# A transformer block on one core: heads loaded one by one, uses booked further behind transfers, program order from V on, and splits ahead of additions

## The chip, the cores and the metric

The kernel runs on one core of a Trainium2 chip. The metric is the device time of one execution in microseconds (us), as a median over runs. Five engines have a part in it. In the profile TensorE is PE, with its weight loads listed apart as PEld; VectorE is DVE, ScalarE is ACT, GpSimd is POOL, and SyncE, which here does nothing but issue DMAs, is SP. "SPq" and "ACTq" are rows of an engine's DMA issues.

## What is computed

```python
xn = layernorm(x)                                   # x: 2048 x 576
q, k, v = heads(xn @ wqkv)                          # 32 heads of 18
p = softmax(mask(q @ k.T * 18 ** -0.5))             # a row sees itself and the 255 before
s = (p @ v) @ wo
z = gelu(xn @ w_in)                                 # 2 x 2304 channels
z1, z2 = z[:, :2304], layernorm(z[:, 2304:])
g = silu((z1 * (w_sp @ z2 + b_sp)) @ w_out)         # w_sp: 2048 x 2048, along the sequence
out = x + s * g
```

Both branches take the normalised x. All data is fp32.

## The kernel before

**Number format.** Every large product is made of fp32r halves: `split` (lines 111 to 113) writes a rounded upper half with ACT (L112) and the remainder with DVE (L113), and TensorE multiplies upper by upper, upper by lower and lower by upper.

**Stages.** (1) Q and K: x is normalised and transposed, `qk_chunk` multiplies, and SP stores the rows to `st_d` in DRAM. (2) V (`v_matmuls`, L465 to L473): sixteen row blocks, two PSUM buffers `vps`; ACT copies each to `ve` (L472) and issues its store itself (L473). (3) z2 (L678): six column parts `pc` of sixteen row blocks `s`; ACT makes the Gelu (L698), and its own queue stores two blocks at a time to `z2_d`. Beside it GpSimd makes sums and differences of the quarters of w_sp (`sp_combos`, L610 to L627) for the spatial stage, which is a product of 2 x 2 blocks with seven multiplications instead of eight; they go to `sc_d`. The weights of the next column part come in three pieces (`load_z2`, `pieces`): each piece is loaded, and at the second next row block split. (4) The heads, with z1 between. (5) The spatial product. (6) The product with wo, and the output.

**Heads.** The work is cut into 16 units: four heads and one half of the sequence each. A unit is two pairs of heads; a pair has one of five SBUF slots `att0` to `att4`, with the first head in partitions 0 to 63 and the second in 64 to 127: a part with two heads' Q, and a part with both heads' K. `load_pair` issues eight DMAs for a pair, four for each head (L361 to L364, from `st_d`). Both pairs that follow, the second pair of the next unit and the first of the one behind it, are loaded in one go at the start of each unit. Three streams are interleaved on TensorE:
- `row_max` (a matmul L394, then DVE's maximum L398) runs some 42 steps ahead and finds each row's maximum, which goes through DRAM (`m_d`) into the slot.
- `scores` (L526) takes the items of the unit, each a block of keys of one head: 32 in a unit of the first half, 40 in the second. ACT takes the exponential into `pt` (L530). `pv` multiplies by V (L549).
- `fill` hands out the matmuls of z1 (L447), 14 to a group of 512 columns. ACT copies a group to `z1o` (L450), SP stores it (L376). The weights of the next 128 channels come with `load_z1` (L425, tile `z1raw`) and are split into `z1wh` and `z1wl` (L483 in the profile, where the jobs are called) when they are booked in `extras`.

`finish` ends a unit: a row of the PV product holds the denominators. SP brings them to a tile `den` (L598), DVE inverts (L574), SP sends them to `r_d` (L575) and spreads them over the partitions (`rp`, L579), DVE multiplies (L583), and SP stores four heads to `o_d` (L589).

**Order.** In these stages the kernel sets the order itself. `manual_schedule` names the engines that run in the order of the program; from V through z2 these are PE, POOL and DVE (`ENGINES`), while ACT and SP are put in an order by the compiler's own schedule; in the heads they are all five (`HEADS`). Inside that, `after(ns, fn)` books a piece of work a number of nanoseconds on, by a clock that `spend` moves by an estimate for each matmul; `tick` issues what has come due. `extras` is a list of jobs for DVE and ACT, of which `extra` issues some. An engine does what it was given strictly in this order, so a late input stops everything behind it.

**Spatial.** 168 steps m: three groups g of 384 channels, seven products n, eight steps s. A step is 18 matmuls into six PSUM banks `acc` (L964). SP loads a tile of w_sp or of its combinations (`load_w`, tile `spr`, L205), ACT and DVE split it into `sph` and `spl` and the z2 tile into `zh` and `zl` (`split_step`, L210 in the profile), two steps ahead. `pump` loads z2 blocks (`zr`) and normalises them (ACT, and DVE at L159 to L165). When a product ends (s = 7) `evict` adds or copies the six banks; the additions of the second product are at L913, the copies of the first at L925. It also books in `lazy` the loads of z1 (`z1t`, L881), their Gelu (L889), the products with the gate and the stores to `y_d`; `run_lazy(4)` issues four of these in each step. All five engines follow the program here.

One place a sentence can't say, the end of a spatial step:

```python
            if s == 7:
                evict(g, n)
            load_w(m + 4)
            if m:
                split_step(m + 2)
...
            pump(2 if len(units) > 8 and (m < 4 or m % 3 == 0) else 1)
            run_lazy(4)
```

Of the kernel before, what the change touches and what calls it, by code (L numbers as in the profile page):

```python
# [44 lines left out]
GAP = 7  # L45
TAIL = 66
HEAD = 6
# [14 lines left out]
def kernel(  # L62
# [163 lines left out]
    with ExitStack() as early:  # L226
# [108 lines left out]
        with ExitStack() as ph:  # L335
# [17 lines left out]
            def load_pair(p):  # L353
                u, a = divmod(p, 2)
                g, half = UNITS[u]
                q0 = half * HS
                k0, kn = (0, HS) if half == 0 else (HS - 256, HS + 256)
                for j in (2 * a, 2 * a + 1):
                    h, b = 4 * g + j, 64 * (j % 2)
                    q, k = f32(q_of(u, j)), f32(k_of(u, j))  # L360
                    sp.dma_start(q[b:b + 36, :], st_d[0, 0:36, h, q0:q0 + HS])  # L361
                    sp.dma_start(k[b:b + 18, :kn], st_d[1, 18:36, h, k0:k0 + kn])
                    sp.dma_start(q[b + 36:b + 56, :], st_d[0, 18:38, h, q0:q0 + HS])
                    sp.dma_start(k[b + 18:b + 54, :kn], st_d[1, 0:36, h, k0:k0 + kn])  # L364

            waiting, seen = [], []
# [69 lines left out]
            def z1_matmuls():  # L436
                nxt = z1_first.pop()
                for f in range(FH // P):
# [3 lines left out]
                    for c in range(NC):  # L442
# [3 lines left out]
                        for n, (w, r) in enumerate(pl):  # L446
# [7 lines left out]
                            if c == 1 and n == 7 and f + 1 < FH // P:  # L454
                                extras.append(nxt[2])
# [111 lines left out]
            def finish(u, ou):  # L567
# [5 lines left out]
                def invert():  # L573
                    dve.reciprocal(den, den)  # L574
                    after(600, lambda: sp.dma_start(r_d[u].rearrange("h (a b) -> (h a) b", b=HS // 32), den))  # L575
                    after(2800, spread)

                def spread():
                    sp.dma_start(rp, r_d[u].unsqueeze(1).to_broadcast([4, 32, HS]))  # L579
                    after(9500, lambda: queue([divide]))  # L580
# [5 lines left out]
                def store():  # L586
                    for i in range(4):
# [11 lines left out]
                after(3600, lambda: queue([invert]))  # L599

            def sp_combos(stack):
# [13 lines left out]
                for n, (q, cs) in enumerate(steps):  # L615
# [9 lines left out]
                    yield  # L625
                    for k, t in enumerate((a22, a11, a21, a12)):
                        sp.dma_start(sc_d[k, q, :, cs], t)  # L627
# [3 lines left out]
            order.enter_context(tc.manual_schedule(engines=ENGINES))  # L631
            with ExitStack() as gate:
                def load_z2(pc):
# [26 lines left out]
                for pc in range(6):  # L660
# [7 lines left out]
                    if pc == 3:  # L668
                        load_pair(0)
                        load_pair(1)  # L670
                    if pc == 4:
                        load_pair(2)
                    for s in range(NS):
# [8 lines left out]
                        if (pc * NS + s) % 3 != 2:  # L682
# [33 lines left out]
            with ExitStack() as heads:  # L716
# [19 lines left out]
                for u in range(NU):  # L736
                    g, half = UNITS[u]
                    tick()
                    if u == NU - 1:
# [12 lines left out]
                        for q in range(8):  # L752
                            prep.append(partial(act.activation, z0[:, q], z0[:, q], AF.Identity,
                                                scale=rstd2[:, q:q + 1], bias=nmr2[:, q:q + 1]))
# [7 lines left out]
                    for t, (s, j) in enumerate(items):  # L762
                        f = (t + 1) / len(items)
                        scores(u, *s, j)
# [20 lines left out]
                        if u == NU - 1 and t >= 12 and prep:  # L785
# [9 lines left out]
                fill(1)  # L795
                work.close()
                wpools[2] = open_pool(sets, "w2", side="right")
                load_w(2)
                fill(12)
# [29 lines left out]
    with ExitStack() as ph:  # L829
# [124 lines left out]
        for m, (g, n, s) in enumerate(order_sp):  # L954
# [11 lines left out]
            if s == 7:  # L966
                evict(g, n)
# [6 lines left out]
            run_lazy(4)  # L974
            if s == 5:
# [154 lines left out]
```

## Time and profile before

| what | before |
|---|---|
| median of 3 runs (lowest, highest) | 2070.53 us (2068.66, 2072.85) |
| the profiled execution: its time, its span | 2066.54 us, 2064.8 us |
| mean granted TensorE clock | 0.979 |
| busy: PE, DVE, ACT, POOL | 94%, 51%, 43%, 14% |
| busy share of the DMA engines by SP's and ACT's own queues | 54.0%, 3.7% |
| Q and K up to | 174 us |
| V up to | 211 us |
| z2 up to | 457 us |
| heads and z1 up to | 1045 us |
| spatial product up to | 1796 us |

The span runs from the first to the last instruction of the profiled execution. A row of a timeline names the start, the length, the engine and the source line; what stands in brackets is the idle time of the engine ahead of that instruction, and what ended it. Tile names lose their numbers there: `att` is any of the five slots, `acc` any PSUM bank, `b` any of the buffers `b0` to `b5`.

### The profile page before, as it was taken

To read this page: it belongs to the slowest core of one execution; us is meant where nothing else is said; L and a number is where in the kernel's file an instruction comes from. 1 tells how busy PE (TensorE), PEld (TensorE's weight loads), DVE (VectorE), ACT (ScalarE), POOL (GpSimd) and SP (SyncE) were. 2 spreads that over 40 slices of the span, in tenths; PEclk is the share of its full clock that TensorE was granted. 3 is DMA by queue.
4 is the path that set the end of the run, shared out by engine and by line. 5 is a ranking of instruction groups with operands and counts; after the bars stand their busy time and mean duration, and the time that the engine had idled before them with its cause. 6 is when DMAs were issued, how large, how long until landed. Compare 5 with 4: busy or idle time off the path is not lost.

```text
span 2064.8 us, 30616 instructions
## 1 busy us (share of the span) xinstructions
PE 1948.8 (94%) x11096; PEld 1672.1 (81%) x11096; DVE 1058.7 (51%) x2258; ACT 897.4 (43%) x1655; POOL 285.6 (14%) x362
## 2 busy tenths in 40 slices
PE   6999999998988889989998998999999999999998
PEld 5888999996766667767586887788888877999998
DVE  6411323365655556556236675667775666533231
ACT  4212222224554446556655555555655344432221
POOL 5001556102222222223300000000000000000000
PEclk9999999999999999999999999999999999999999
DMA  8655899234454545545456667665784466764451
GB/s 244 172 143 168 289 337 327 100 96 120 127 138 113 132 122 144 139 124 141 142 194 200 209 231 245 215 218 197 262 278 159 153 211 228 243 209 141 151 161 54
DMA packets 218983, 375.57 MB, mean 182 GB/s; under 512 B 43216, under 2 KB 115792, under 8 KB 218704
## 3 DMA queue, kind: packets, MB, share of 16 engines
q1 hardware_dynamic: 201168, 344.94, 54.0%
q10 hardware_dynamic: 17664, 28.69, 3.7%
q8 instruction: 87, 1.43, 0.3%
q14 instruction: 64, 0.52, 0.1%
HBM read 260.45 MB, written 112.83 MB: 181 GB/s over the span
## 4 chain that ended last, share of the span: by engine, by line
PE 73%; DMA 14%; DVE 7%; ACT 3%; issue 2%; SPq 1%; ACTq 0%; POOL 0%; DVEq 0%; POOLq 0%
PE acc L964 24%; PE po L1057 11%; PE mm L678 10%; PE mm L447 8%; PE mm L306 5%; PE tps L526 3%; PE ops L549 3%; PE sp L394 3%; DMA att<-st_d 3%; PE vps L465 2%; DMA z1t<-z_d 2%; DMA den<-ou 2%; DMA z1raw<-in_w_z_dram 1%; DVE spl L210 1%; PE wops L1027 1%
## 5 line engine op out<-in xcount | busy, mean ns | idle before, releaser
L964 PE MATMUL acc<-sph,zh 128*128 128x512 f32 x1008 | 397.5, 394 | 22.0 <-ACT sph L210 22.0
L964 PE MATMUL acc<-spl,zh 128*128 128x512 f32 x1008 | 398.1, 395 | 5.9 <-DVE spl L210 5.8
L964 PE MATMUL acc<-sph,zl 128*128 128x512 f32 x1008 | 396.1, 393 | 0.0
L398 DVE CUSTOM_DVE_ANT_0 junk<-sp,band 128x384 bf16<-128x384 f32 (+1 forms) x512 | 272.1, 538 | 181.9 <-PE sp L394 178.2
L530 ACT ACTIVATE pt<-tps 128x384 f32<-128x384 f32 (+2 forms) x576 | 247.3, 439 | 176.6 <-PE tps L526 163.6
L447 PE MATMUL mm<-b,z1wh 128*128 128x512 f32 x648 | 258.7, 409 | 0.0
L964 PEld LDWEIGHTS acc<-sph,zh 128*128 128x128 f32 x1008 | 191.9, 190 | 65.1 <-ACT sph L210 24.9
L964 PEld LDWEIGHTS acc<-spl,zh 128*128 128x128 f32 x1008 | 191.7, 190 | 50.7 <-DVE spl L210 11.0
L210 DVE TENSOR_TENSOR spl<-spr,sph 128x1024 fp32r<-128x1024 f32 x166 | 203.2, 1224 | 57.3 <-ACT sph L210 56.5
L964 PEld LDWEIGHTS acc<-sph,zl 128*128 128x128 f32 x1008 | 191.9, 190 | 39.8
L526 PE MATMUL tps<-att 128*128 128x384 f32 (+1 forms) x576 | 193.7, 336 | 23.6 <-ACT pt L530 21.7
L394 PE MATMUL sp<-att 128*128 128x384 f32 (+1 forms) x512 | 177.1, 346 | 33.6 <-DVE mx L398 26.5
L678 PE MATMUL mm<-z2wh,b 128*128 128x384 f32 x720 | 194.0, 337 | 3.6 <-ACT zt L698 3.6
L210 ACT ACTIVATE sph<-spr 128x1024 fp32r<-128x1024 f32 x166 | 173.9, 1048 | 36.3 <-DMA spr<-sc_d 25.1
L210 ACT ACTIVATE zh<-b 128x384 fp32r<-128x384 f32 x144 | 74.9, 520 | 195.8 <-PE acc L964 195.8
L210 DVE TENSOR_TENSOR zl<-b,zh 128x384 fp32r<-128x384 f32 x144 | 80.1, 556 | 151.5 <-ACT zh L210 151.4
L1057 PE MATMUL po<-b,yh 128*128 128x288 f32 x896 | 152.4, 292 | 0.0
L526 PEld LDWEIGHTS tps<-att 128*128 128x128 f32 x576 | 112.6, 195 | 48.1 <-ACT pt L530 35.7
L447 PEld LDWEIGHTS mm<-b,z1wh 128*128 128x128 f32 x648 | 126.1, 195 | 27.9 <-issue 7.2
L533 POOL TENSOR_SCALAR_AFFINE_SELECT pt<-pt 128x512 f32<-128x512 f32 x128 | 83.1, 649 | 462.4 <-ACT pt L530 462.4
L447 PE MATMUL mm<-b,z1wl 128*128 128x512 f32 x360 | 147.0, 408 | 0.0
L699 DVE BATCH_NORM_STATS2 st<-zt 128x6 f32<-128x384 f32 x96 | 53.5, 560 | 170.9 <-ACT zt L698 170.9
(150 smaller groups left out, 2913.7 us busy)
## 6 DMA issues: line engine op xcount, KB each, us to landing
spr<-sc_d SPq DMA_DIRECT2D x96, 512.0 KB
spr<-in_w_sp_dram SPq DMA_DIRECT2D x72, 512.0 KB
zr<-z_d SPq DMA_DIRECT2D x136, 192.0 KB
st_d<-qkhl SPq DMA_DIRECT2D x72, 256.0 KB
z_d<-zt ACTq DMA_DIRECT2D x48, 384.0 KB
z_d<-z1o SPq DMA_DIRECT2D x72, 256.0 KB
z1t<-z_d SPq DMA_DIRECT2D x72, 256.0 KB
y_d<-z1t SPq DMA_DIRECT2D x72, 256.0 KB
```

The costliest lines, as they stand in the source:

```text
L210: job()
L306: pe.matmul(ps, w, r, start=n == 0, stop=n == len(pl) - 1)
L394: pe.matmul(ps[:, :w], q_of(u, j)[:, i * P:(i + 1) * P], k_of(u, j)[:, k0:k0 + w], start=True, stop=True)
L398: dve.tensor_tensor_reduce(out=junk[:, :w], in0=ps[:, :w], in1=band[:, m0:m0 + w], scale=1.0, scalar=-3.0e38, op0=ALU.add, op1=ALU.max, ac ...
L447: pe.matmul(ps, w, r, start=n == 0, stop=n == len(pl) - 1)
L526: pe.matmul(ps[:, :m * P], k_of(u, j)[:, (kb - base) * P:(kb - base + 1) * P], q_of(u, j)[:, (a - lo) * P:(a - lo + m) * P], start=True, s ...
L530: act.activation(pt[:, j, d0:d0 + n * P], ps[:, (qa - a) * P:(qa - a + n) * P], AF.Exp, scale=scale)
L533: pool.affine_select(out=pt[:, :, 0:P], in_=pt[:, :, 0:P], pattern=[[0, 4], [1, P]], compare_op=ALU.is_ge, fill=0.0, base=0, channel_multi ...
L549: pe.matmul(o_ps[c][32 * j:32 * j + 32, (lo - 4 * c) * P:(hi - 4 * c + 1) * P], vgs[u][:, kb - k0, j * VW:j * VW + 32], pt[:, j, (lo - kb) ...
L678: pe.matmul(ps[:, :ZW], r, wt, start=n == 0, stop=n == len(pl) - 1)
L964: pe.matmul(acc[j], z[:, ps], w[:, cs], start=s == i == 0 and n in OPENS, stop=s == 7 and i == 2, skip_group_check=True)
L1057: pe.matmul(po[i][:, a, :288], y[:, i * P:(i + 1) * P], w[:, a * 288:(a + 1) * 288], start=f == 0 and m == 0, stop=f == NF - 1 and m == 2)
```

## The change

1. `load_head` takes the place of `load_pair`. Of the same four heads that a unit loads, each is now issued ahead of an item of its own, t = 0, 4, 10 and 16 (`LOAD_AT`): first the two heads of the second pair of the next unit, then the two of the first pair of the unit behind it.
2. Bookings. The reciprocal is booked 8000 ns instead of 3600 behind the PV product's end (except in the last two units), the denominators' store 900 instead of 600 and the spreading 3000 instead of 2800 ns behind it, the division 12000 instead of 9500 (9000 in the last two units). The split of the next z1 weights is booked seven matmuls later. Sixteen instead of six z1 matmuls stand ahead of the first unit (`HEAD`).
3. From V on ACT and SP run in the order of the program too (`HEADS` instead of `ENGINES`). V's loop calls the pieces of z2's first weights itself; the pieces of the others are loaded two ahead of their split (three tiles in hand instead of one at a time); `sp_combos` has one more `yield` ahead of its stores and is called at seven of eight row blocks instead of two of three.
4. In the last unit z0 is normalised by DVE instead of ACT and these jobs begin at t = 8 instead of 12. Behind the heads the program fills until the last but one unit's stores are issued (`stored`).
5. In the spatial product `evict` moves from the front of a step's work to its end.

```diff
-            def load_pair(p):
-                u, a = divmod(p, 2)
+            def load_head(u, j):
                 g, half = UNITS[u]
...
-                            if c == 1 and n == 7 and f + 1 < FH // P:
+                            if c == 2 and n == 0 and f + 1 < FH // P:
                                 extras.append(nxt[2])
...
-                    after(600, lambda: sp.dma_start(r_d[u].rearrange("h (a b) -> (h a) b", b=HS // 32), den))
-                    after(2800, spread)
+                    after(900, lambda: sp.dma_start(r_d[u].rearrange("h (a b) -> (h a) b", b=HS // 32), den))
+                    after(3000, spread)
...
-                    after(9500, lambda: queue([divide]))
+                    after(12000 if u < NU - 2 else 9000, lambda: queue([divide]))
...
-                after(3600, lambda: queue([invert]))
+                after(8000 if u < NU - 2 else 3600, lambda: queue([invert]))
...
                     pool.tensor_tensor(a12, a12, a11, ALU.subtract)
                     yield
+                    yield
                     for k, t in enumerate((a22, a11, a21, a12)):
                         sp.dma_start(sc_d[k, q, :, cs], t)
...
-            order.enter_context(tc.manual_schedule(engines=ENGINES))
+            order.enter_context(tc.manual_schedule(engines=HEADS))
...
+                    def piece(c):
+                        raw = f32(zw.tile([P, 5, P], F32R, name=("z1wh", "z1wl")[c % 2]))
+                        sp.dma_start(raw, w_z2[:, :, pc * ZW + c * P:pc * ZW + (c + 1) * P])
+                        return raw
+
                     def pieces():
+                        raws = [piece(0)]
+                        yield
+                        raws.append(piece(1))
+                        yield
                         for c in range(3):
                             cs = slice(c * P, (c + 1) * P)
-                            raw = f32(zw.tile([P, 5, P], F32R, name=("z1wh", "z1wl")[c % 2]))
-                            sp.dma_start(raw, w_z2[:, :, pc * ZW + c * P:pc * ZW + (c + 1) * P])
+                            split(wh[:, :, cs], wl[:, :, cs], raws[c])
+                            if c == 0:
+                                raws.append(piece(2))
                             yield
-                            split(wh[:, :, cs], wl[:, :, cs], raw)
-                            yield
...
-                for _ in nxt[2]:
-                    pass
-                for _ in vm:
-                    pass
+                for n, _ in enumerate(vm):
+                    if n % 28 == 7:
+                        next(nxt[2], None)
...
-                        if (pc * NS + s) % 3 != 2:
+                        if (pc * NS + s) % 8 != 7:
                             next(combos, None)
...
-                    for p in (2 * u + 3, 2 * u + 4):
-                        if p < 2 * NU:
-                            load_pair(p)
+                    heads_at = {LOAD_AT[i]: (u + 1 + i // 2, (2, 3, 0, 1)[i]) for i in range(4)}
...
                         f = (t + 1) / len(items)
+                        if t in heads_at and heads_at[t][0] < NU:
+                            load_head(*heads_at[t])
                         scores(u, *s, j)
...
-            if s == 7:
-                evict(g, n)
             load_w(m + 4)
             if m:
                 split_step(m + 2)
...
             run_lazy(4)
+            if s == 7:
+                evict(g, n)
```

Three places show what it moves. The first is SP in the fifth unit, which starts at 595.18 us in the trace. Before, these rows stand behind twelve more head loads: `att_1207` is a slot, `z1raw` the next z1 weights, `den` the denominators of the unit before.

```order
L361 DMA att_1207<-st_d 36x1024
L362 DMA att_1207<-st_d 18x1024
L363 DMA att_1207<-st_d 20x1024
L364 DMA att_1207<-st_d 36x1024
L425 DMA z1raw<-in_w_z_dram 128x640
L376 DMA z_d<-z1o 128x512
L598 DMA den<-ou 128x1x32
L575 DMA r_d<-den 128x32
```

After, with the last load of the first head at the top (source lines of the changed kernel, one less here):

```order
L363 DMA att_1206<-st_d 36x1024
L424 DMA z1raw<-in_w_z_dram 128x640
L589 DMA o_d<-ou 18x1024 x4
L375 DMA z_d<-z1o 128x512
L360 DMA att_1206<-st_d 36x1024
L361 DMA att_1206<-st_d 18x1024
L362 DMA att_1206<-st_d 20x1024
L363 DMA att_1206<-st_d 36x1024
L598 DMA den<-ou 128x1x32
```

The z1 weights now stand behind four head loads and the denominators behind eight, where both stood behind sixteen; and the output stores of an earlier unit, `o_d`, have come between the two heads of the pair.

The second place is DVE where the spatial product's second product ends. Before, `cb` are the six additions, `zl` and `spl` the lower halves for a step ahead, `b` a z2 tile.

```order
L161 TENSOR_TENSOR b_11539<-b_11304,z_10577 128x384
L913 TENSOR_TENSOR cb<-acc_11028,b_11025 128x512
L913 TENSOR_TENSOR cb<-acc_11029,b_11025 128x512
L913 TENSOR_TENSOR cb<-acc_11030,b_11025 128x512
L913 TENSOR_TENSOR cb<-acc_11031,b_11025 128x512
L913 TENSOR_TENSOR cb<-acc_11032,b_11025 128x512
L913 TENSOR_TENSOR cb<-acc_11033,b_11025 128x512
L210 TENSOR_TENSOR zl<-b_11304,zh 128x384
L210 TENSOR_TENSOR spl<-spr,sph 128x1024
```

After (in the changed kernel's own line numbers, where L211 is the splits and L925 the additions):

```order
L211 TENSOR_TENSOR zl<-b_11292,zh 128x384
L211 TENSOR_TENSOR spl<-spr,sph 128x1024
L162 TENSOR_TENSOR b_11539<-b_11292,z_10577 128x384 x2
L925 TENSOR_TENSOR cb<-acc_11028,b_11025 128x512
L925 TENSOR_TENSOR cb<-acc_11029,b_11025 128x512
L925 TENSOR_TENSOR cb<-acc_11030,b_11025 128x512
L925 TENSOR_TENSOR cb<-acc_11031,b_11025 128x512
L925 TENSOR_TENSOR cb<-acc_11032,b_11025 128x512
L925 TENSOR_TENSOR cb<-acc_11033,b_11025 128x512
L211 TENSOR_TENSOR zl<-b_11292,zh 128x384
L211 TENSOR_TENSOR spl<-spr,sph 128x1024
```

The same six additions now stand behind the split and the normalisations of their own step, and ahead of the next step's split.

The third place is ACT where Q and K end and V begins. `qkhl` is the upper half of a Q or K group, `ve` the copy of a V group, `v_d` its store; `att_1205` and `z2wh` receive z2's weights. Before:

```order
L112 ACTIVATE qkhl<-mm 128x512 x4
L472 ACTIVATE ve<-vps 128x16x18 x2
L473 DMA v_d<-ve 128x621
L112 ACTIVATE qkhl<-mm 128x512
L112 ACTIVATE z2wh<-z1wl 128x5x128
L472 ACTIVATE ve<-vps 128x16x18 x2
L473 DMA v_d<-ve 128x621
L112 ACTIVATE att_1205<-z1wh 128x5x128
```

After:

```order
L471 ACTIVATE ve<-vps 128x16x18 x2
L472 DMA v_d<-ve 128x621
L113 ACTIVATE qkhl<-mm 128x512 x13
L113 ACTIVATE att_1205<-z1wh 128x5x128
L471 ACTIVATE ve<-vps 128x16x18 x2
L472 DMA v_d<-ve 128x621
L471 ACTIVATE ve<-vps 128x16x18 x2
L472 DMA v_d<-ve 128x621
```

The copies of V groups between the last Q and K groups are gone, and the copy of z2's first piece stands ahead of two V groups.

More of the change, by code (lines that the diff above doesn't have):

```diff
@@ L45 @@
 GAP = 7
+LOAD_AT = (0, 4, 10, 16)
 TAIL = 66
-HEAD = 6
+HEAD = 16
 _SHARE = [18 + 0.4 * (i >= 8) for i in range(16)]
@@ L357, in load_pair @@
                 k0, kn = (0, HS) if half == 0 else (HS - 256, HS + 256)
[L358 to L366, printed above, removed]
+                h, b = 4 * g + j, 64 * (j % 2)
+                q, k = f32(q_of(u, j)), f32(k_of(u, j))
+                sp.dma_start(q[b:b + 36, :], st_d[0, 0:36, h, q0:q0 + HS])
+                sp.dma_start(k[b:b + 18, :kn], st_d[1, 18:36, h, k0:k0 + kn])
+                sp.dma_start(q[b + 36:b + 56, :], st_d[0, 18:38, h, q0:q0 + HS])
+                sp.dma_start(k[b + 18:b + 54, :kn], st_d[1, 0:36, h, k0:k0 + kn])
+            waiting, seen, stored = [], [], set()
             clock = 0.0
@@ L586, in store @@
                 def store():
+                    stored.add(u)
                     for i in range(4):
@@ L668 @@
                     if pc == 3:
-                        load_pair(0)
-                        load_pair(1)
+                        for j in range(4):
+                            load_head(0, j)
                     if pc == 4:
-                        load_pair(2)
+                        for j in range(2):
+                            load_head(1, j)
                     for s in range(NS):
@@ L752 @@
                         for q in range(8):
-                            prep.append(partial(act.activation, z0[:, q], z0[:, q], AF.Identity,
-                                                scale=rstd2[:, q:q + 1], bias=nmr2[:, q:q + 1]))
+                            prep.append(partial(dve.tensor_scalar, z0[:, q], z0[:, q], rstd2[:, q:q + 1],
+                                                nmr2[:, q:q + 1], ALU.mult, ALU.add))
                         prep += split_jobs(0) + split_jobs(1)
-                    for p in (2 * u + 3, 2 * u + 4):
-                        if p < 2 * NU:
-                            load_pair(p)
+                    heads_at = {LOAD_AT[i]: (u + 1 + i // 2, (2, 3, 0, 1)[i]) for i in range(4)}
                     steps = steps_of(half)
@@ L784 @@
                             load_v(u + 1)
-                        if u == NU - 1 and t >= 12 and prep:
+                        if u == NU - 1 and t >= 8 and prep:
                             prep.pop(0)()
@@ L795 @@
                 fill(1)
+                while NU - 2 not in stored:
+                    fill(1)
+                    extra(1)
                 work.close()
@@ L798 @@
                 load_w(2)
-                fill(12)
+                fill(10)
                 split_step(2)
```

## The prediction

> **What bounds the kernel now.** The page first: TensorE (PE) is busy for 94% of the span, the others for half or less, so the time is PE's work plus the time in which PE waits or runs slowly.
>
> ```profile
> span 2064.8 us, 30616 instructions
> PE 1948.8 (94%) x11096; PEld 1672.1 (81%) x11096; DVE 1058.7 (51%) x2258; ACT 897.4 (43%) x1655; POOL 285.6 (14%) x362
> ```
>
> The windows view by stage: start:end, length, busy time of PE, PEld, DVE, ACT and POOL, then granted PE clock, DMA share, GB/s. The stages are z2, the heads and the spatial product:
>
> ```profile
> 211.00:457.00 246.00, 242.42 (x1387) 240.96 (x1386) 94.42 (x213) 56.31 (x112) 94.46 (x70) 0.99 0.66 233
> 457.00:1045.00 588.00, 528.73 (x3475) 406.74 (x3474) 315.62 (x1071) 321.36 (x747) 153.09 (x240) 0.96 0.49 132
> 1045.00:1796.00 751.00, 723.12 (x3183) 595.33 (x3182) 491.36 (x690) 391.60 (x582) 0.00 (x0) 0.98 0.65 216
> ```
>
> PE idles 3.6, 59.3 and 27.9 us there. The view of waits, over the whole span, says for what (total, times, longest); the rows of DVE and ACT, over the heads, name what stands behind two of them:
>
> ```profile
> PE sp L394 <- DVE mx L398: 26.5, 14, 4.4
> PE acc L964 <- ACT sph L210: 22.0, 6, 5.6
> PE tps L526 <- ACT pt L530: 21.7, 13, 6.1
> PE sp L394 <- DMA att<-st_d: 6.9, 7, 2.4
> PE acc L964 <- DVE spl L210: 5.8, 10, 0.8
> PE vps L465 <- ACT ve L472: 2.6, 1, 2.6
> DVE den L574 <- DMA den<-ou: 50.1, 9, 18.0
> ACT z1wh L483 <- DMA z1raw<-in_w_z_dram: 20.7, 5, 7.1
> ```
>
> One such stall, in the unit that starts at 595.18, by the timeline (start, length, engine, line; in brackets idle time before it and its releaser). SyncE (SP) issues sixteen head loads (the dots), then the z1 weights, and only then the denominators; DVE stands at the reciprocal, row maxima queue behind it, PE stops:
>
> ```profile
> 595.18 0.34 PE L526 MATMUL tps<-att 128*128 128x384 f32 x1
> 595.00 0.33 SPq L361 DMA_DIRECT2D att<-st_d  x1
> ...
> 605.44 0.57 SPq L598 DMA_DIRECT2D den<-ou  x1
> 610.41 0.35 DVE L574 RECIPROCAL den<-den 128x32 f32<-128x32 f32 x1 [4.61 <-DMA den<-ou]
> 611.23 0.69 PE L394 MATMUL sp<-att 128*128 128x384 f32 x1 [3.75 <-DVE mx L398]
> ```
>
> A stall costs more than its length. After 2.84 us of idling the granted clock is half for the next 3.4 us; around a stall of 1.79 us it is full:
>
> ```profile
> 508.45 0.56 PE L394 MATMUL sp<-att 128*128 128x384 f32 x1 [2.84 <-DVE mx L398]
> 508.62:512.03 3.41, 3.41 (x10) 3.04 (x11) 1.39 (x6) 1.56 (x4) 0.00 (x0) 0.50 0.57 137
> 542.67 0.44 PE L394 MATMUL sp<-att 128*128 128x384 f32 x1 [1.79 <-DVE mx L398]
> 541.00:546.00 5.00, 3.33 (x17) 3.00 (x18) 3.38 (x13) 2.88 (x7) 0.89 (x3) 1.00 0.66 193
> 641.74:648.56 6.82, 3.56 (x10) 3.17 (x11) 1.26 (x5) 3.07 (x7) 1.22 (x2) 0.50 0.28 76
> ```
>
> So a long stall loses 1.7 us more. From the stage clocks: heads 0.04 x 588 = 23 us withheld, spatial 0.02 x 751 = 15. Part of that falls on idle time (half of it in the last row, none in the 508 row), so I count four fifths: 19 and 12 us. In z2 it is 0.01 x 246 = 2, and V's one stall of 2.6 us adds about 1. With that stall, 93 us of idling and 34 of slow clock lie between V and the end of the spatial product; the rest of the kernel the change hardly touches.
>
> **The change, heads.** *Reciprocal.* It is booked 4.4 us later, and only eight of the sixteen head loads now stand in front of its DMA. DVE waited 50.1 us for it in nine places, 18.0 of them in the last unit, where nothing needs DVE: the other eight are 4.0 us on average (4.61 above). The two shifts together are more, so this stall goes, and with it nearly all of the 26.5 us. The z1 split moves seven z1 matmuls back, and its load is issued ahead of most head loads instead of behind all sixteen: of the 20.7 us that ACT waited for it, at most 7.1 at once, nothing should remain, and of PE's 21.7 little. HEAD = 16 covers the table switch at the start. In the last unit eight normalisations go from ACT to DVE, which has no row maxima left. The second pair of each unit, now loaded at t = 10 and 16, is first read near t = 24 of 32, eight items or some 8 us later, longer than any landing below: no cost. PE's own order is the same from the last head to the spatial product, so the wait for the last output stores costs nothing either.
>
> *What is late next.* The first row maximum of an even head needs the K rows of both heads of its pair: the slot's K tile is read on all 128 partitions. Here PE waited for the eighth load of the unit:
>
> ```profile
> 707.36 0.33 SPq L361 DMA_DIRECT2D att<-st_d  x1
> ...
> 711.31 0.29 SPq L364 DMA_DIRECT2D att<-st_d  x1
> 717.59 0.41 PE L394 MATMUL sp<-att 128*128 128x384 f32 x1 [1.22 <-DMA att<-st_d]
> 603.65 0.28 PE L394 MATMUL sp<-att 128*128 128x256 f32 x1
> 498.80 3.07 DMA att<-st_d
> L583 DVE TENSOR_TENSOR ou<-ou,rp 128x1024 f32<-128x1024 f32 x15 | 18.8, 1250 | 0.0
> ```
>
> It is needed 8.5 us after the unit's start (603.65 against 595.18). After the change the pair's second head stands behind t = 4 and, in seven units (2 to 8), behind the four output stores, which wait for the divide. That is two row maxima into the unit: 2 us, near 1 until DVE is there, 1.25 for the divide, 1.5 for four SP issues at 0.33 us and the gaps between, 1.4 for the head's own: its last load is issued about 7 us in. A head load lands 3.07 us (the chain of waits) to 6.2 us (711.31 to 717.59, a full queue) after issue; with few in flight I take 3.5, nearer the lower row. Arrival 10.4, so 1.9 us of stall (0.8 to 4). Seven times that is 13 us; about four units with only a z1 store between lose 0.7 each, 3 us. Three of the seven fall on the slow clock, 5 us. Nine more us for small waits (the pair's maxima, the start, the last unit). So 25 us idle and 5 slow remain of 59 + 19: **48 us gained** (bounds 26, if all seven stall 4 us and lose the clock, and 66, if none does).
>
> By the Trainium skill (TensorE: Matmul & The Clock Gate, "Why this matters for your kernels") only PE gaps over about 3 us bring the half clock back; the 2.84 us row here is already shorter. By that rule the 5 us would be free.
>
> **Spatial.** Today the additions at the end of a product stand ahead of the next split on DVE and ACT. Six copies hold ACT, then SP's z1 load comes late, the Gelu waits for it, the next split stands behind, PE stops:
>
> ```profile
> 1074.67 4.00 ACT L925 ACTIVATE t<-acc 128x512 f32<-128x512 f32 x6 [2.31 <-PE acc L964]
> 1085.47 1.84 SPq L881 DMA_DIRECT2D z1t<-z_d  x4
> 1090.57 1.32 ACT L889 ACTIVATE z1t<-z1t 128x512 f32<-128x512 f32 x2 [5.49 <-DMA z1t<-z_d]
> 1093.30 0.80 PE L964 MATMUL acc<-sph,zh 128*128 128x512 f32 x1 [3.03 <-ACT sph L210]
> ```
>
> SP loads a spatial tile when the split three steps earlier has freed its buffer, so whatever delays a split delays SP. With the split in front, the additions (4.0 us here) delay a split that is needed one step (18 matmuls, 4.1 us) later than now. The stalls right behind the copies and the 5.8 us on spl should go; those that come from z1 loads six steps behind the additions keep the same distance from load to Gelu, and I leave half. That is 9 us idle and 4 slow left of 28 + 12: **27 us gained** (12 to 38). A price on the other side: the additions now wait for the step's normalisations, and the next product's third bank waits for them; at most some 0.5 us at twelve places, counted in the 9.
>
> **V and z2.** ACT and SP keep program order. Rows of ACT:
>
> ```profile
> 173.04 0.60 ACT L112 ACTIVATE qkhl<-mm 128x512 fp32r<-128x512 f32 x1 [2.96 <-PE mm L306]
> 176.27 0.71 ACT L472 ACTIVATE ve<-vps 128x288 f32<-128x288 f32 x2 [2.00 <-PE vps L465]
> 177.39 0.74 ACT L112 ACTIVATE att<-z1wh 128x640 fp32r<-128x640 f32 x1 [0.40 <-ACT ve L472]
> ```
>
> Two V groups fill both PSUM buffers before the last QK matmul, and ACT then does 0.60 + 0.74 + 0.71 before one is free: 2.2 us stall, in the place of those that go. In z2 the halves of w_sp are combined at the pace of before (seven of eight calls, but four instead of three to a step), by GpSimd, which is idle most of the stage; I take 3 us idle and 2 slow. Of 6 + 3, 2 us are gained (bounds 7 gained, and the last rival).
>
> Sum: 48 + 27 + 2 = 77 us. The profiled execution took 2066.5 us (its span and 1.7 around it), 4 under the median of the runs, 2070.5: 2066.5 - 77 = 1989.5, and as a median 1993.5, which I give as **1993 us**.
>
> **Rivals.**
> *All of it goes* (1963 us). The second head arrives in time; 10 + 2 us left in the heads, 3 in spatial, 5 in z2: 107 us. For it: the 603.65 row does not wait. Against: the stores in between.
> *Spatial stays as it is* (2020): load and Gelu only move together by one step, and SP is held by something else. 50 us gained.
> *The second head is late in every unit* (2041). At the full-queue latency it stalls 3 us and the clock drops, 4.7 us in 15 units, 70 us: the heads gain nothing, the rest 29. The Trainium skill (DMA: Bandwidth & Descriptors, "Rules for kernel authors") would have a DMA issued early and waited for late, which speaks against head by head; the 717.59 row bears it out where the queue is full.
> *Slower* (2103). In z2 SP, in program order, issues loads of spatial rows only when the store from the same buffer has landed, and a weight piece behind that:
>
> ```profile
> 267.11 6.56 DMA sc_d<-a
> 184.16 8.00 DMA z1wh<-in_w_z_dram
> ```
>
> A piece is split four row blocks after its load (246 us / 96 = 2.56 us each, 10.2 us). If SP has nothing in hand, 6.6 + 8.0 = 14.6 us stop ACT for 4.4; with a queue as full as in the rows above 1 us more, so up to 5.5 us, which PE takes over where its two PSUM buffers are full, and 1.7 of slow clock, for 15 pieces: 108 us lost against 75 gained. It decides when SP runs less than 2 us ahead of PE there; it needs nothing from PE but free buffers, so it should run ahead.
>
> **How the numbers follow.** Forecast 0.56 (own range 1975 to 2012), all goes 0.18, spatial unchanged 0.11, second head late 0.08, slower 0.05, and 0.02 that gains and losses cancel. Range 1958 to 2032: it takes in the second and third case and leaves out the last ones. About 0.2% is what a measurement of this kernel can tell. Faster 0.92, within 0.2% 0.02, slower 0.06.
>
> **What would show it.** DVE's wait for den and ACT's for z1raw near zero; PE's wait for att<-st_d up, in units 2 to 8, at the first maximum of the third head; acc waits below 10 us; a 2 us gap where QK ends. Wrong if PE waits on ACT by several us in z2, or if the idle time of the heads stays above 40 us.

## The result, and the profile after

| | before | after |
|---|---|---|
| median of 4 runs (lowest, highest) | 2069.94 us (2068.66, 2072.85) | 2038.51 us (2032.33, 2042.78) |
| profiled execution: time, span | 2066.54, 2064.8 us | 2042.78, 2041.0 us |

The ratio is 0.9844, with a 95% interval of 0.9815 to 0.9873. The kernel became 31.4 us faster; 77 were forecast, and the median lies above the range (1958 to 2032). The profiled execution is the slowest of its four; between the two spans lie 23.8 us.

A stage is taken here from the last matmul of the one before it to its own last (the heads end at the first spatial matmul; before, the last spatial matmul ends at 1775.3 us, and the 1796 of the first table takes in the start of the next stage). "Idle" is the sum of TensorE's idle times in the timeline, "slow" half of its busy time in windows at half clock:

| stage: length (idle, slow), us | before | after | forecast gain | gain |
|---|---|---|---|---|
| Q, K and V | 210.2 | 209.4 | | 0.8 |
| z2 | 245.7 (3.6, 1.7) | 254.0 (8.2, 4.2) | 2, with V | -8.4 |
| heads | 589.3 (59.3, 18.9) | 553.4 (35.1, 11.5) | 48 | 36.0 |
| spatial | 730.1 (27.9, 12.0) | 727.3 (27.1, 10.8) | 27 | 2.8 |
| wo and output | 284.3 (0.3, 0) | 291.8 (1.1, 0) | 0 | -7.4 |

The gains add up to the 23.8. Each stage time is of one execution. Where a run below leaves a stage's code as it was before the change, that stage took 242.6 to 245.7 us in z2 (four executions), 586.1 to 589.3 in the heads (two) and 730.1 to 732.8 in the spatial product (four); where it leaves it as changed, 252.1 to 257.1 (seven), 547.4 to 557.0 (eight) and 723.4 to 727.3 (seven). The windows view of the changed kernel, for z2, the heads and the spatial stage; the granted clock of the heads is up from 0.96, that of z2 down from 0.99:

```profile
209.40:463.40 254.00, 245.81 (x1386) 242.96 (x1386) 93.54 (x212) 59.18 (x116) 93.75 (x70) 0.98 0.71 236
463.40:1016.80 553.40, 518.26 (x3481) 401.72 (x3480) 321.35 (x1080) 317.14 (x740) 155.06 (x240) 0.98 0.52 141
1016.80:1744.10 727.30, 700.20 (x3027) 574.05 (x3026) 479.30 (x674) 384.84 (x574) 0.00 (x0) 0.98 0.66 216
```

The view of waits of the changed kernel (total, times, longest). The denominators are waited for only once, in the last unit (before 50.1 us), the z1 weights hardly (20.7), row maxima for 3.0 (26.5). Head loads have come up from 6.9 to 23.5. The spatial product waits as long as before, but for other work: 12.9 us for the upper half of the split (22.0), and 8.7 us for additions, which TensorE did not wait for at all before:

```profile
ACT z1t L901 <- DMA z1t<-z_d: 38.2, 17, 7.3
PE sp L393 <- DMA att<-st_d: 23.5, 10, 3.6
PE acc L976 <- ACT sph L211: 12.9, 4, 6.3
DVE den L573 <- DMA den<-ou: 9.2, 1, 9.2
PE acc L976 <- DVE cb L925: 8.7, 2, 6.1
PE mm L687 <- ACT zt L707: 7.8, 4, 4.0
PE acc L976 <- DVE spl L211: 5.4, 8, 0.8
PE sp L393 <- DVE mx L397: 3.0, 6, 0.6
ACT z1wh L482 <- DMA z1raw<-in_w_z_dram: 2.3, 3, 1.1
PE vps L464 <- ACT ve L471: 1.9, 1, 1.9
```

The stall that the prediction foresaw in the heads, in the timeline of the unit that starts at 591.47: the division, SP's four stores that wait for it, then the second head, whose last load is issued 7.2 us into the unit and read 4.8 us later. Below it a stall of 2.08 us with the window at half clock that follows:

```profile
593.28 1.22 DVE L582 TENSOR_TENSOR ou<-ou,rp 128x1024 f32<-128x1024 f32 x1
594.53 1.41 SPq L589 DMA_DIRECT2D o_d<-ou  x4
596.43 1.47 SPq L360 DMA_DIRECT2D att<-st_d  x1
...
598.66 0.33 SPq L363 DMA_DIRECT2D att<-st_d  x1
603.42 0.36 PE L393 MATMUL sp<-att 128*128 128x256 f32 x1 [3.32 <-DMA att<-st_d]
732.74 0.41 PE L393 MATMUL sp<-att 128*128 128x384 f32 x1 [2.08 <-DMA att<-st_d]
734.19:737.60 3.41, 3.41 (x12) 3.03 (x11) 1.70 (x6) 1.59 (x4) 1.22 (x2) 0.50 1.05 194
```

The first spatial stall. SP's loads of z2 blocks wait 9.4 us for buffers, so the last two loads of z1 go out at 1070; ACT reaches their Gelu at once, waits, and the next split stands behind it. One stall of 6.3 us has taken the place of 3.0 and 3.4:

```profile
1060.56 9.41 SPq L147 DMA_DIRECT2D zr<-z_d  x4
1070.03 0.90 SPq L893 DMA_DIRECT2D z1t<-z_d  x2
1073.05 0.63 ACT L901 ACTIVATE z1t<-z1t 128x512 f32<-128x512 f32 x1 [4.79 <-DMA z1t<-z_d]
1075.80 0.63 ACT L901 ACTIVATE z1t<-z1t 128x512 f32<-128x512 f32 x1 [2.13 <-DMA z1t<-z_d]
1076.75 1.04 ACT L211 ACTIVATE sph<-spr 128x1024 fp32r<-128x1024 f32 x1
1077.84 0.80 PE L976 MATMUL acc<-sph,zh 128*128 128x512 f32 x1 [6.32 <-ACT sph L211]
```

And z2's longest. The trace gives the DMAs of SP and ACT one of eight semaphores in turn. ACT's store at 325.47 has the semaphore of the w_sp load eight DMAs ahead of it, the last of four that SP issues only from 316.68 on; ACT stands for 8.2 us, then TensorE has no free PSUM buffer:

```profile
316.68 2.59 SPq L610 DMA_DIRECT2D a<-in_w_sp_dram  x4
325.47 0.37 ACTq L710 DMA_DIRECT2D z_d<-zt  x1
325.96 0.87 ACT L707 ACTIVATE zt<-mm 128x384 f32<-128x384 f32 x2 [8.18 <-DMA a<-in_w_sp_dram]
326.50 0.69 PE L687 MATMUL mm<-z2wh,b 128*128 128x384 f32 x1 [3.96 <-ACT zt L707]
```

### The profile page after: what moved, and what is told of

The parts are those of the page before. It is cut to its first block, busy times and chain, and to the rows that moved or that the text cites. A ratio compares the mean times of both kernels' runs of the same rounds, so it can differ in the third digit from the quotient of the medians.

```text
span 2041.0 us, 30608 instructions
## 1 busy us (share of the span) xinstructions
PE 1945.1 (95%) x11096; PEld 1673.9 (82%) x11096; DVE 1064.5 (52%) x2266; ACT 892.2 (44%) x1647; POOL 287.0 (14%) x362
## 4 chain that ended last, share of the span: by engine, by line
PE 74%; DMA 14%; DVE 3%; SPq 3%; ACT 2%; issue 2%; POOL 1%; ACTq 0%; DVEq 0%; POOLq 0%
PE acc L976 28%; PE po L1069 11%; PE mm L446 10%; PE mm L307 5%; PE mm L687 4%; PE tps L525 4%; DMA sc_d<-a 4%; PE sp L393 4%; DMA att<-st_d 4%; PE ops L548 3%; PE vps L464 3%; PE wops L1039 1%; DMA a<-in_w_sp_dram 1%; DMA z1t<-z_d 1%; DMA spr<-in_w_sp_dram 1%
## 5 line engine op out<-in xcount | busy, mean ns | idle before, releaser
L976 PE MATMUL acc<-sph,zh 128*128 128x512 f32 x1008 | 397.1, 394 | 21.7 <-ACT sph L211 12.9
L211 DVE TENSOR_TENSOR spl<-spr,sph 128x1024 fp32r<-128x1024 f32 x166 | 203.1, 1223 | 65.3 <-ACT sph L211 64.5
L393 PE MATMUL sp<-att 128*128 128x384 f32 (+1 forms) x512 | 173.4, 339 | 28.8 <-DMA att<-st_d 23.5
L211 ACT ACTIVATE sph<-spr 128x1024 fp32r<-128x1024 f32 x166 | 173.9, 1048 | 30.1 <-DMA spr<-sc_d 25.2
L211 ACT ACTIVATE zh<-b 128x384 fp32r<-128x384 f32 x144 | 75.3, 523 | 231.0 <-PE acc L976 230.9
L211 DVE TENSOR_TENSOR zl<-b,zh 128x384 fp32r<-128x384 f32 x144 | 80.0, 555 | 154.3 <-ACT zh L211 154.2
L687 PEld LDWEIGHTS mm<-z2wh,b 128*128 128x128 f32 x720 | 132.9, 191 | 10.7 <-ACT zt L707 10.7
L687 PE MATMUL mm<-z2wl,b 128*128 128x384 f32 x400 | 135.4, 339 | 0.0
```

The lines of the kernel that those rows point to most:

```text
L211: job()
L393: pe.matmul(ps[:, :w], q_of(u, j)[:, i * P:(i + 1) * P], k_of(u, j)[:, k0:k0 + w], start=True, stop=True)
L687: pe.matmul(ps[:, :ZW], r, wt, start=n == 0, stop=n == len(pl) - 1)
L976: pe.matmul(acc[j], z[:, ps], w[:, cs], start=s == i == 0 and n in OPENS, stop=s == 7 and i == 2, skip_group_check=True)
```

## The experiments

Medians are of four runs where an interval is given with them, and the ratio is to the kernel before on the same chip. Line numbers in the views are those of each kernel.

**Spatial: additions put back in front, in the changed kernel.**

```diff
+            if s == 7:
+                evict(g, n)
             load_w(m + 4)
...
             run_lazy(4)
-            if s == 7:
-                evict(g, n)
```

> The changed kernel with the additions put back in front of the step's split. In the changed kernel the spatial stage idles 27.1 us on TensorE, before it idled 27.9. Theory A (ScalarE's Gelu on z1 stands one step behind its load, whichever way the additions stand, and holds the next split): stage idle 24 to 32 us, the time within 5 us of the changed kernel. Rival B (the order matters: it took the old stalls away and put new ones, additions late for the third PSUM bank, in their place): the 8.7 us of waits for the additions go, the 7 us and 10 us stalls behind the copies at the start of the first two groups come back; about the same sum but in the old places. Rival C (the additions late for the bank are a pure loss): idle 18 to 20 us, 10 us faster.

2050.13 us (0.9911, 0.9877 to 0.9946). The stage took 731.7 us, 4.4 more than in the changed kernel, idle 25.2, slow 17.6, with the stalls in the old places: 3.4 and 3.1 us in the first group, 5.4 and 2.8 in the second. TensorE waits for no addition, and the waits of ACT for z1 and of TensorE for the split are again near those before the change (62.7 and 22.0 us):

```profile
ACT z1t L901 <- DMA z1t<-z_d: 59.1, 21, 11.0
...
PE acc L976 <- ACT sph L211: 20.4, 7, 5.4
```

That is B's picture; by A's "within 5 us" it is the stage alone that fits. Rival C falls.

**Gelus one step later, in the changed kernel.**

```diff
             for n in range(6):
                 lazy.append(one(c, p))
...
+            lazy.extend([lambda: None] * 4)
             for n in range(6):
                 lazy.append(lambda n=n: act.activation(ts[n], ts[n], AF.Gelu_apprx_tanh))
```

> The changed kernel with four empty entries in the list of small jobs between the loads of z1 and their Gelus, so that each Gelu is issued one step (4.1 us) later behind its load. Theory A: ScalarE's waits for z1 (38 us) fall below 15, the spatial idle time from 27.1 to under 12 us, slow clock from 10.8 to under 5: 15 to 22 us faster than the changed kernel. Rival B or C (the position of the additions, the tiles of w_sp coming late): the idle time stays above 20 us, under 6 us faster.

2030.92 us (0.9821, 0.9790 to 0.9852). ACT's wait for z1 nearly went, but the idle time fell only from 27.1 to 22.0 (slow 6.5), the stage to 717.5; theory A alone, which asked for under 12 us idle, does not hold. The waits for additions grew, as the waits of this kernel and its longest stall in the timeline show:

```profile
PE acc L977 <- DVE cb L926: 13.9, 3, 6.1
...
ACT z1t L902 <- DMA z1t<-z_d: 2.7, 3, 1.4
```

```profile
1426.89 1.06 ACT L211 ACTIVATE sph<-spr 128x1024 fp32r<-128x1024 f32 x1 [1.52 <-DMA spr<-sc_d]
1427.98 1.22 DVE L211 TENSOR_TENSOR spl<-spr,sph 128x1024 fp32r<-128x1024 f32 x1 [1.36 <-ACT sph L211]
1430.25 3.07 DVE L926 TENSOR_TENSOR cb<-acc,t 128x512 f32<-128x512 f32 x5
1431.08 0.77 PE L977 MATMUL acc<-sph,zh 128*128 128x512 f32 x1 [6.12 <-DVE cb L926]
```

A tile of w_sp lands late, the split waits for it, and the additions, which need none of it, stand behind the split; the next product's third bank waits for them.

**Both.** The additions in front and the Gelus later, the two edits above together.

> Both: additions in front of the split again, Gelus one step later. Theory A: as good as the Gelus alone within 5 us, spatial idle under 14 us. Rival B (with the load waits gone the position decides): worse than the Gelus alone by 8 us or more if the split behind the additions is what stalls, better if the late bank is.

2028.26 us (0.9803, 0.9771 to 0.9836); the stage 708.7 us, idle 12.6, slow 6.8. The waits for additions are 0.5 us:

```profile
PE acc L977 <- ACT sph L211: 6.9, 4, 2.5
PE acc L977 <- DVE spl L211: 5.1, 6, 1.3
ACT z1t L902 <- DMA z1t<-z_d: 2.3, 2, 1.6
PE acc L977 <- DVE cb L926: 0.5, 1, 0.5
```

The four cases side by side: with the Gelu close behind its load, 731.7 us with the additions in front and 727.3 behind; with the Gelu later, 708.7 in front and 717.5 behind. The move gains 4.4 us in the one and loses 8.8 in the other. Both theories were half right: the Gelus cost most, and behind them the place of the additions decides, the other way round than in the change.

**z2: head loads spread, in the changed kernel.**

```diff
-                    if pc == 3:
-                        for j in range(4):
-                            load_head(0, j)
-                    if pc == 4:
-                        for j in range(2):
-                            load_head(1, j)
                     for s in range(NS):
+                        if pc == 3 and s in (0, 3, 6, 9):
+                            load_head(0, s // 3)
+                        if pc == 4 and s in (0, 3):
+                            load_head(1, s // 3)
```

> The changed kernel with the six head loads of the z2 stage spread out, one every third row block, instead of sixteen and eight DMAs in one go. In the changed kernel z2 idles 8.2 us and loses 4.2 to the slow clock, where ScalarE's store of z2 stands for 8.2 and 6.4 us behind these loads. Theory D (a store on ScalarE waits for the DMA eight back in the program's order, here a head load that SyncE has yet to issue): z2 idle under 3 us, 6 to 10 us faster than the changed kernel. Rival E (program order as such, or the combinations at four calls to a step, hold ScalarE): idle stays above 5 us, under 3 us faster.

2045.40 us (0.9884, 0.9847 to 0.9921). z2 took 264.1 us and idled 17.2, twice as much. Theory D falls: it is not the burst. (Its premise was half wrong: the wait of 8.2 us was for a load of w_sp, as the view above shows, and not for a head load.) With SP's head loads between ACT's stores in more places there were more stalls.

**The compiler's order again in V and z2, in the changed kernel; and the pace of the combinations, with program order kept.**

```diff
-            order.enter_context(tc.manual_schedule(engines=HEADS))
+            order.enter_context(tc.manual_schedule(engines=ENGINES))
```

> The changed kernel, but from V through z2 ScalarE and SyncE are again in the order of the compiler's schedule (only the set of engines is put back; pieces, combinations and their pace as changed). In the changed kernel V idles 1.9 us and z2 8.2, with 4.2 of slow clock; before it was 2.6, 3.6, and 3.4 of slow clock in both together. Theory F (program order of the two engines costs z2: ScalarE's store takes its turn among the transfers behind loads that SyncE has not issued): z2 idle under 4.5 us, z2 5 to 9 us shorter. Rival G (the pace of the combinations costs it): z2 idle stays above 7 us.

```diff
                     yield
-                    yield
                     for k, t in enumerate((a22, a11, a21, a12)):
...
-                        if (pc * NS + s) % 8 != 7:
+                        if (pc * NS + s) % 3 != 2:
                             next(combos, None)
```

> The changed kernel with the combinations of w_sp as before (no second empty step ahead of their stores, called at two of three row blocks). Rival G: z2 idle falls from 8.2 to under 5 us. Theory F: it stays between 7 and 13 us, the time within 4 us of the changed kernel.

The first: 2028.33 us (0.9807, 0.9784 to 0.9831), z2 243.8 us long, idle 3.2, no slow clock; z2 ends at 449.8 instead of 463.4. The second: 2037.99 us (0.9843, 0.9816 to 0.9870), z2 254.8, idle 9.6. Theory F holds and G falls: program order for ACT and SP costs some 10 us in z2 and, by this run, 3 ahead of it. That the price comes by way of the shared turns is read from the rows at 316.68 and 325.47; no run takes the turns apart from the order. The row of the first kernel's windows view for z2 has the full clock again:

```profile
206.00:449.80 243.80, 240.57 (x1387) 239.33 (x1386) 94.49 (x212) 56.35 (x112) 93.67 (x70) 1.00 0.67 235
```

**Heads: output stores behind the second head; and the second head at t = 1 besides.**

```diff
-                    after(1500, store)
+                    after(4000, store)
```

> The changed kernel with the four output stores booked 4000 ns behind the division instead of 1500, so that in units 2 to 8 they stand behind the second head's loads and not ahead of them. Theory H (these stores, which wait for the division, make the second head late): the waits of the row maxima for head loads fall from 23.5 us to 8 to 13, and with four of the seven slow windows in the heads gone the stage gets 10 to 16 us shorter. Rival I (the second head is late by its own place at t = 4 and a landing of nearly 5 us): 18 us or more of these waits stay, under 5 us gained.

```diff
-LOAD_AT = (0, 4, 10, 16)
+LOAD_AT = (0, 1, 10, 16)
```

> The same with the second head loaded ahead of the unit's second item (t = 1) instead of its fifth. Theory H and rival I both: the waits for head loads fall below 6 us, the heads take 14 to 22 us less than in the changed kernel, unless rival J holds: eight loads in one go bring the wait for the z1 weights or the denominators back (ScalarE or VectorE waiting over 10 us for them), and under 8 us are gained.

With the stores moved: 2018.18 us (0.9743, 0.9729 to 0.9758); heads 528.5 us, 24.9 less than in the changed kernel, idle 18.8, slow 1.7. With t = 1 too: 2014.99 (0.9725, 0.9706 to 0.9744), heads 527.4, which is no clear gain more. Theory H holds, and with more than was expected of it; rival I falls, and J does not show (z1 weights 2.3 us, denominators in the last unit alone). Of the 23.5 us of waits for head loads the first leaves:

```profile
PE sp L393 <- DMA o_d<-ou: 5.3, 5, 1.8
...
PE sp L393 <- DMA att<-st_d: 4.5, 4, 2.7
```

**Loads alone and bookings alone, in the kernel before.** The first takes `load_head` and `LOAD_AT`, the second five numbers:

```diff
-                    after(600, lambda: sp.dma_start(r_d...
-                    after(2800, spread)
+                    after(900, lambda: sp.dma_start(r_d...
+                    after(3000, spread)
-                    after(9500, lambda: queue([divide]))
+                    after(12000 if u < NU - 2 else 9000, lambda: queue([divide]))
-                after(3600, lambda: queue([invert]))
+                after(8000 if u < NU - 2 else 3600, lambda: queue([invert]))
-                            if c == 1 and n == 7 and f + 1 < FH // P:
+                            if c == 2 and n == 0 and f + 1 < FH // P:
```

> The kernel before with the loads head by head alone (t = 0, 4, 10, 16); bookings, order and spatial stage as before. Before, the heads take 589 us, with VectorE waiting 50 us for the denominators (18 of them in the last unit, where nothing needs it) and ScalarE 21 for the z1 weights; after the whole change 553, and those waits 9 and 2. Theory M (the transfers ahead in SyncE's queue were the cause, so the loads do most of it): the waits fall to under 25 and 6 us, the heads take 555 to 572 us. Rival N (the later bookings do it): denominators still over 35 us, heads over 580.

> The kernel before with the later bookings alone (reciprocal, its store, spreading, division, split of the z1 weights); pairs loaded as before. Theory M: denominators still over 30 us, heads over 575 us. Rival N: denominators under 20 us, and as the second head of a pair isn't late here, heads of 545 to 560 us, as good as after the whole change or better.

Loads alone: 2029.01 us (0.9809, 0.9783 to 0.9834), heads 551.3. Bookings alone: 2022.48 (0.9781, 0.9750 to 0.9812), heads 541.3. The loads alone do what M says, the bookings alone nearly what N says; so neither is the one cause, and each part alone takes the wait for denominators off the path. The waits of the loads alone, then of the bookings alone:

```profile
DVE den L573 <- DMA den<-ou: 16.7, 1, 16.7
...
PE sp L393 <- DMA att<-st_d: 6.9, 5, 1.8
```

```profile
DVE den L574 <- DMA den<-ou: 21.4, 7, 14.4
...
PE sp L394 <- DMA att<-st_d: 5.8, 4, 2.3
```

Each alone is better for the heads than or as good as both (553.4). Only together do they put the later division, and the stores behind it, between the two heads of a pair: 5.8 and 6.9 us of waits for head loads in the single kernels, 23.5 in the changed one.

**The output product: one more matmul ahead of seven of its eight parts; and the kernel before once more.**

```diff
             po = [outp.tile([P, 2, 512], F32, name=f"po{i}") for i in range(2)]
+            if n:
+                pe.matmul(po[0][:, 0, :128], wos[0][0][:, :P], wos[0][0][:, :P], start=True, stop=True, skip_group_check=True)
```

> The changed kernel with one small matmul more (128 columns; its result is overwritten) ahead of each of the last seven of the eight parts of the output product. Before, the matmuls of that product started every 130 ns, after the change every 133.3 (one in four takes 140), which costs 5.8 us, in the same code. Theory K (it hangs on where the instructions stand in TensorE's stream, which the changed number of waits ahead of them has moved): parts differ, some at 130, some at 133.3 ns. Rival L (where the tiles lie, or what the other engines do): all eight parts at 133.3 ns.

> The kernel before, once more with a profile. In its first profile the matmuls of the output product started every 130.0 ns; in every other kernel so far every 133.3 (5.8 us in 1728 matmuls). Theory P (it is a property of that one execution): 133.3 ns now, the stage 230.4 us. Theory Q (it is a property of this program): 130.0 ns again, 224.6 us. The heads should idle 59 us again, the spatial stage 28, within 3 us.

With the matmul: 2044.09 us, one run; every part at 133.3 to 133.5 ns, so K falls as far as it was tried. The kernel before once more: 2063.91 us, the output product 230.4 us. P holds: the 224.6 belong to the one execution that was profiled first. The group of its matmuls on the two executions of the kernel before, the first on top:

```profile
L1057 PE MATMUL po<-b,yh 128*128 128x288 f32 x896 | 152.4, 292 | 0.0
```

```profile
L1057 PE MATMUL po<-b,yh 128*128 128x288 f32 x896 | 155.8, 296 | 0.0
```

The heads idled 57.8 and the spatial stage 29.9 us here, near the first profile.

**All that helped, in the changed kernel; and the Gelus one more step later** (the edits of z_engines, h_store, h_early and s_front_gelu; then eight empty entries for four).

> The changed kernel with all that helped alone: the compiler's order for ScalarE and SyncE in V and z2, the second head at t = 1 with the output stores behind it, the additions in front of the split, the Gelus one step later. If the stages don't depend on each other: 13.7 us less in V and z2, 26 in the heads and 18.7 in the spatial stage than in the changed kernel's profile, 58 in all, 1978 to 1985 us. If time saved in one stage is given back in the next: over 1990.

> The fastest kernel so far (all that helped) with the Gelus one more step later, eight empty entries instead of four. If loads of z1 still hold ScalarE anywhere, the spatial idle time falls from 14.2 us to under 10, 3 to 6 us faster; if what is left comes from the tiles of w_sp, no change within 2 us.

1983.52 us (0.9594, 0.9565 to 0.9624) and 1983.93 (0.9583, 0.9554 to 0.9612). The stages add up: 243.7, 526.2 and 707.1 us in the first, within the time expected; its windows for z2, heads and spatial stage:

```profile
207.40:451.10 243.70, 241.83 (x1387) 240.91 (x1386) 94.35 (x212) 56.47 (x112) 93.62 (x70) 0.99 0.68 235
451.10:977.30 526.20, 510.56 (x3480) 396.07 (x3480) 321.59 (x1080) 317.31 (x740) 153.41 (x240) 0.99 0.55 148
977.30:1684.40 707.10, 692.91 (x3027) 567.67 (x3025) 481.44 (x674) 385.34 (x574) 0.00 (x0) 1.00 0.67 222
```

The eight entries change nothing (spatial 706.8 us): what is left there are tiles of w_sp.

## Why the prediction was wrong

Of the 53 us that are missing between the profiled spans, 24 are in the spatial product, 12 in the heads, 10 in V and z2 and 7 behind them.

**Spatial, 27 forecast, 2.8 measured: the step that failed.** The prediction left 9 of 28 us idle, with the price of late additions in the 9. "The stalls right behind the copies and the 5.8 us on spl should go" and "those that come from z1 loads ... I leave half". The stalls behind the copies were stalls on z1 too: the chain that the prediction itself quoted runs from the late z1 load over the Gelu to the split, and the copies only made it later. The distance from load to Gelu is one step whichever way the additions stand. ACT still waited 38.2 us for z1, TensorE still 12.9 us for the upper half of the split and 5.4 (before 5.8) for the lower. Taking the Gelus apart from their loads gains 9.8 us, and 23 with the additions in front (731.7 to 708.7). And the price on the other side was given as "at most some 0.5 us at twelve places": that counts the normalisations, not the split in front of them, which waits for a DMA. It was 2.5 and 6.1 us at two places, 8.7 in all, and took back what the split's waits had fallen by. The rival "spatial stays as it is" had the reason right in the main, with 0.11.

**V and z2, 2 forecast, 7.6 lost** (8.4 in z2, 0.8 won ahead of it)**.** The 2.2 us stall at the end of Q and K came as 1.91. In z2 the prediction watched a piece of the weights and a chance of 0.05 that SP falls behind by much; it left out that ACT's stores share the eight turns with SP's DMAs, so that ACT can be held by an SP that is late by a little. TensorE's 7.8 us of waits for ACT there are a sign of being wrong that the prediction had named. The last rival had program order as its cause too, but by way of the weights and at ten times the price: z_engines shows 10 us in z2.

**Heads, 48 forecast, 36 measured.** The chain went as told: denominators and z1 weights off the path, the second head the next to be late, behind the stores, 10.4 us forecast into the unit and 12.0 in the one shown (598.66 plus 4.8, less 591.47). Two terms were mis-sized: a landing of 4.8 us where 3.5 was taken from the nearer row, and ten stalls of 2.4 us on average, five of them with half clock behind them, where the prediction had seven of 1.9, four of 0.7 and three slow windows. Moving the stores away is worth 24.9 us, where the prediction had 13 + 5 for it; the heads without it would have come to 61, near its bound of 66. That two edits, each of which alone takes the stall away, would spoil each other was in the text only as a stall, not as a reason to cost the parts one by one.

By the Trainium skill (TensorE: Matmul & The Clock Gate, "Why this matters for your kernels") there should be no idle gaps of TensorE above about 3 us, or the clock falls to half; the row at 732.74 shows a half-clock window after 2.08 us, so the trace doesn't agree. The 1.9 us of stall that the prediction took for free of it in four of seven units was too near this. The rule of the Trainium skill to issue a DMA early and wait for it late (DMA: Bandwidth & Descriptors, "Rules for kernel authors") agrees with h_store, where the second head's loads no longer stand behind the division (24.9 us).

**The output, 0 forecast, 7.4 lost, 5.8 of them in its product.** The 5.8 are no property of either kernel: a second execution of the kernel before had 230.4 us too. By two executions this is how far a term that "the change hardly touches" can be off; z2 differed by 2.8 us and V by 3.0 between the same two.

The measured time is close to the 2041 of the rival "second head late in every unit", but by luck, for the sum is another: the heads did gain. What stays open: why one execution ran the output product at 130 ns a matmul, and 4.4 us of the heads' gain, which are neither idle time nor slow windows. They are no scatter: the heads less both took 510.6 to 511.9 us in the kernel before (two executions), the loads alone and the bookings alone, and 506.8 to 508.0 in all twelve other runs; which part of the change does it was not tried.

## What to carry to other kernels

A wait on a DMA blocks everything behind it on its engine, so when work is moved behind such a wait, its price is that DMA's lateness and not the duration of what it is moved behind. Before a stall is put down to the work that stands ahead of it, follow it to the transfer at its start and count the steps between issue and use: if the edit leaves that number as it is, the stall stays. And when two edits mend the same stall, cost each alone; here either was better for the heads than, or as good as, both.

## What had not been expected of the hardware

The same program ran the same 1728 matmuls once every 130.0 ns and once every 133.3, without idle time and at the same granted clock of 1.00.

The length of a gap does not decide by itself whether half clock follows. In s_front_gelu a gap of 1.76 us brought it and one of 3.19 us did not:

```profile
737.85 0.41 PE L393 MATMUL sp<-att 128*128 128x384 f32 x1 [1.76 <-DMA att<-st_d]
738.88:742.29 3.41, 3.41 (x12) 3.02 (x11) 1.13 (x4) 1.83 (x5) 1.22 (x2) 0.50 1.03 176
375.12 0.44 PE L687 MATMUL mm<-z2wh,b 128*128 128x384 f32 x1 [3.19 <-ACT zt L707]
370.24:377.07 6.83, 3.64 (x21) 3.32 (x20) 1.02 (x2) 0.87 (x2) 5.10 (x4) 1.00 0.89 265
```

In each of the sixteen traces all half-clock windows start on one grid of 3.413 us. From 180 us to the end of the output product, none of the 8186 steps of these grids at full clock in which TensorE idled for less than 0.44 of the step (1.50 us) was followed by half clock, and all 151 were in which it idled for more than 0.56 (1.91 us); in between it was 19 of 76. The gap of 1.76 us lies within one step, the one of 3.19 us is split into 1.72 and 1.47.

A head load was read 4.8 us after its issue (598.66 to 603.42) with no more than nine DMAs issued in the 4.5 us up to it.
